# Soft-MoE tail of an attention kernel: the last two blocks of combine weights built before the first expert product, and half of the second expert layer issued in 16-instruction parts between the output tiles

## The chip, the core and the metric

The kernel runs on one core of a Trainium2 chip. The core has a tensor engine (PE; its weight loads are listed apart as PEld), a vector engine (DVE), a scalar engine (ACT), a general engine (POOL), and a queue engine (SP) that issues the kernel's transfers to 16 DMA engines. Each engine works through its own instructions in program order; engines wait for one another through semaphores. The metric is the device time of one execution in microseconds (us).

## The reference

Eight batches of eight heads, 576 tokens of 64 features. A causal softmax attention is mixed with a memory read-out by a gate; the result, 4608 rows of 512, goes into a soft mixture of experts: 8 experts, 4 slots each, hidden width 1024. What the change touches is only the end of it:

```python
logits = x @ phi                                  # 4608 x 32
d = softmax over the rows; slot_input = d.T @ x   # 32 x 512
for e in range(E):
    h = np.maximum(slot_input[e] @ w1[e], 0.0)    # 4 x 1024
    slot_out[e] = h @ w2[e]                       # 4 x 512
c = softmax of logits over the 32 slots           # the combine weights
return c @ slot_out                               # 4608 x 512
```

## The kernel before

The first nine tenths of the span run the attention pair by pair and, beside it, the running softmax of the slots. This part is a list of some thousand small steps in a fixed order (`SEQ`); `pin()` ties each engine's instructions to that order, so no planner moves anything. The change leaves this list alone.

The tail begins when the list is through. All of its matrices are small in rows and large in weights, so that it is a stream of expert weights through PE, and then a stream of output tiles to memory:

- `f1(eg, f)` (matmuls on line 937, ReLU on line 940) is one of four quarters of the first layer: expert group `eg` (4 experts), half `f` of the hidden width. 32 matmul instructions into one PSUM tile of the pool `psF` (2 buffers), then one ACT instruction.
- `f1t(eg, f)` (line 945) transposes its result on PE into a tile of `psP` (2 buffers); DVE copies it to `hT` (its row in the profile is the helper's line 357).
- `f2(dh, eg, f, cs_)` (line 954) is a quarter of the second layer for the output half `dh` (256 of the 512 columns), accumulated in one tile of `psF` over the four pairs (eg, f). `cs_` picks chunks of the hidden width: all four chunks are 32 matmul instructions, two are 16. So a quarter can be issued whole or in parts without a change in the instructions.
- `c1(qd)` (lines 960 to 971) makes the combine weights of row block `qd`: a transpose into `psP`, then a chain DVE, DVE, ACT exponential, four DVE. `c2(qd)` (line 975) transposes them back, and ACT copies them into `cT[:, qd]`. Blocks 0 to 6 were done in the list; 7 and 8 are left for the tail.
- `c3(i, j)` splits the combine weights into a high and a low part for the faster matmul type: two ACT casts (rows with the helper's line 354, `w<-cT` or `xk<-cT`) and one DVE subtraction (line 989). `c3(0, j)` takes 8 blocks at once (1024 columns), `c3(1, j)` only the ninth (128). The four tiles of `c3(0, j)` lie where weights of `f1(0, 1)` lay, so they may be written once that product has read them.
- `g1(dh)` (line 996, DVE) scales a finished half of the second layer; `g2(dh)` sums it over the partitions on PE (line 1000) and splits it (ACT cast, DVE line 1002).
- `comb(dh, t4)` makes one output tile of 512 rows by 256 columns: 4 matmuls (line 1011) into two tiles of `psC` (4 buffers), one copied out by ACT and one by DVE (`pc` in their rows), and a transfer of 512 KB to memory on the SP queue (line 1013). There are nine for each half.
- `wload` (line 757) loads one weight tile of 512 KB. 44 of 64 are loaded ahead of the tail; the other 20, all for the second layer, go into the buffers of first-layer weights that have been used (`reload`), so they wait for `f1(0, 0)`, `f1(0, 1)` and `f1(1, 0)`.

PE, ACT and DVE each take the tail's steps in the order of the lines 1015 to 1051: where a call stands in this list fixes the order of its instructions on every engine that it uses.

Of the kernel before, what the change touches and what calls it, by code (L numbers as in the profile page):

```python
# [284 lines left out]
def tile_attn_soft_moe(ctx, tc, q, k, v, M, beta, phi, w1, w2, cst, out):  # L285
# [67 lines left out]
    def act(o, i):  # L353
        nc.scalar.copy(o, i)  # L354
# [393 lines left out]
    def wload(x, pool, name):  # L748
        l, *i, g = order[x]


        if l == 0:
            t = pool.tile([128, 2, 512], F32, name=name)
            nc.sync.dma_start(out=t, in_=w1[4 * i[0] + g, i[1], i[2]])
        else:
            t = pool.tile([128, 4, 256], F32, name=name)
            nc.sync.dma_start(out=t, in_=w2[4 * i[1] + g, i[0], i[2]])
        wt[order[x]] = t
        wslot[order[x]] = (pool, name)
# [173 lines left out]
    def f1(eg, f):  # L933
        ps = psF.tile([128, 512], F32, name="pf")
        for c in range(4):
            for g in range(4):
                nc.tensor.matmul(ps[32 * g:32 * g + 32, :], si[:, c, 32 * (4 * eg + g):32 * (4 * eg + g) + 32],  # L937
                                 wt[0, eg, f, c // 2, g][:, c % 2, :], start=c == 0, stop=c == 3)
        h = hs[eg, f] = par[f].tile([128, 512], F32, name="qp")
        nc.scalar.activation(h, ps, AF.Relu)  # L940

    def f1t(eg, f):
        pt = psP.tile([128, 512], F32, name="pp")
        for x in range(4):
            nc.tensor.transpose(out=pt[:, 128 * x:128 * x + 128], in_=hs[eg, f][:, 128 * x:128 * x + 128], identity=ident)
        dve(hT[:, eg, 4 * f:4 * f + 4, :].rearrange("a x y -> a (x y)"), pt)


    def f2(dh, eg, f, cs_=range(4)):
        if dh not in po:  # L950
            po[dh] = psF.tile([128, 512], F32, name="pf")
        for c in cs_:
            for g in range(4):
                nc.tensor.matmul(po[dh][32 * g:32 * g + 32, 0:256], hT[:, eg, 4 * f + c, 32 * g:32 * g + 32], wt[1, dh, eg, f, g][:, c, :],  # L954
                                 start=(eg, f, c) == (0, 0, 0), stop=(eg, f, c) == (1, 1, 3))


    def c1(qd):
        ps = psP.tile([128, 512], F32, name="pp")
        nc.tensor.transpose(out=ps[:, 0:128], in_=y["lt"][:, qd - 7, :], identity=ident)  # L960
        lk = ps[:, 0:128].rearrange("a (j s) -> a j s", s=32)
        m4 = sml.tile([128, 4], F32, name="m4")
        nc.vector.reduce_max(out=m4, in_=lk, axis=AX.X)
        c = cc[qd] = sml.tile([128, 4, 32], F32, name=("lt", "ex")[qd - 7], bufs=1)
        nc.vector.tensor_tensor(out=c, in0=lk, in1=m4.rearrange("a (j x) -> a j x", x=1).broadcast_to([128, 4, 32]), op=ALU.subtract)
        nc.scalar.activation(c, c, AF.Exp)
        s4 = sml.tile([128, 4], F32, name="s4")
        nc.vector.reduce_sum(out=s4, in_=c, axis=AX.X)
        nc.vector.tensor_scalar(out=s4, in0=s4, scalar1=1e-9, scalar2=None, op0=ALU.add)
        nc.vector.reciprocal(out=s4, in_=s4)  # L970
        nc.vector.tensor_tensor(out=c, in0=c, in1=s4.rearrange("a (j x) -> a j x", x=1).broadcast_to([128, 4, 32]), op=ALU.mult)

    def c2(qd):
        ps = psP.tile([128, 512], F32, name="pp")
        nc.tensor.transpose(out=ps[:, 0:128], in_=cc[qd].rearrange("a j s -> a (j s)"), identity=ident)
        act(cT[:, qd, :], ps[:, 0:128])
# [4 lines left out]
    def c3(i, j):  # L981
        r = slice(32 * j, 32 * j + 32)
        if i == 0:
            pool, name = cslot[j]
            cst4.append(pool.tile([128, 8, 128], F32R, name=name))
        o, w = ((cst4[j], cT[r, 0:8]), (cst8[:, j], cT[r, 8]))[i]
        act(o[0:32], w)
        act(o[64:96], w)
        nc.vector.tensor_tensor(out=o[32:64], in0=w, in1=o[64:96].bitcast(F32), op=ALU.subtract)
# [5 lines left out]
    def g1(dh):  # L995
        nc.vector.tensor_scalar(out=ogs[:, dh], in0=po[dh][:, 0:256], scalar1=dt, scalar2=None, op0=ALU.mult)

    def g2(dh):
        pm = psP.tile([128, 512], F32, name="pp")
        nc.tensor.matmul(pm[:, 0:256], sel, ogs[:, dh], start=True, stop=True)  # L1000
        act(so[0:96, dh], pm[0:96, 0:256])
        nc.vector.tensor_tensor(out=so[64:96, dh], in0=pm[64:96, 0:256], in1=so[64:96, dh].bitcast(F32), op=ALU.subtract)

    def comb(dh, t4):
        pool, name = stage[NQ * dh + t4]
        o = pool.tile([128, 4, 256], F32, name=name)
        for half in range(2):
            ps = psC.tile([128, 2, 256], F32, name="pc")
            for v2 in range(2):
                u = 2 * half + v2  # L1010
                nc.tensor.matmul(ps[:, v2], (cst4[u][0:96, t4, :] if t4 < 8 else cst8[0:96, u, :]), so[0:96, dh], start=True, stop=True)  # L1011
            (act, dve)[half](o[:, 2 * half:2 * half + 2, :], ps)
        nc.sync.dma_start(out=out[512 * t4:512 * t4 + 512, 256 * dh:256 * dh + 256].rearrange("(u a) d -> a u d", a=128), in_=o)

    f1(0, 0)
    f1(0, 1)
    f1t(0, 0)
    c1(7)
    c1(8)
    f1(1, 0)  # L1020
    f1t(0, 1)
    c2(7)
    c2(8)
    f1(1, 1)
    f1t(1, 0)
    c3(0, 0)
    f2(0, 0, 0)
    f1t(1, 1)
    for x, (pool, name) in enumerate(reload):
        wload(nw + x, pool, name)  # L1030
    for j in range(1, 4):
        c3(0, j)
    for j in range(4):
        c3(1, j)
    f2(0, 0, 1)
    f2(0, 1, 0)
    f2(0, 1, 1)
    g1(0)
    f2(1, 0, 0, (0,))
    g2(0)  # L1040
    f2(1, 0, 0, (1, 2, 3))
    for t4 in range(NQ):
        comb(0, t4)
        if t4 == 4:
            f2(1, 0, 1)
    f2(1, 1, 0)
    f2(1, 1, 1)
    g1(1)
    g2(1)
    for t4 in range(NQ):  # L1050
        comb(1, t4)
    pin()
# [13 lines left out]
def build(nc, shapes=None):  # L1066
    dims = [("q", (B, 512, S + 384)), ("k", (B, 512, S)), ("v", (B, NP, 128, 6, 128)), ("M", (B, NP, 128, 160)),
            ("beta", (128, NP, 10)), ("phi", (128, NP, 32)),
            ("w1", (E, 2, 2, 128, 2, 512)), ("w2", (E, 2, 2, 128, 4, 256)), ("cst", (128, CW))]
    args = [nc.dram_tensor(f"in_{n}_dram", s, F32, kind="ExternalInput").ap() for n, s in dims]  # L1070
    args.append(nc.dram_tensor("out_0_dram", (B * S, DM), F32, kind="ExternalOutput").ap())
    with tile.TileContext(nc) as tc:
        tile_attn_soft_moe(tc, *args)
# [44 lines left out]
```

## Time and profile before

| | us |
|---|---|
| median of 3 runs | 483.08 (481.46 to 484.53) |
| the profiled execution, whole | 482.45 |
| its span, first to last instruction | 480.7 |
| start of the tail's first product `f1(0, 0)` | 416.01 |
| first output transfer issued | 450.95 |

The sum in the prediction is made against the profiled execution: what lies outside its span is 482.45 - 480.7 = 1.75 us, and the median of the runs is 0.63 us above it.

In the rows that follow, a line of the timeline has the start in us, the length in us, the engine, the line of the code, the operation, what is written from what is read, the shape, a count, and in brackets the idle time ahead of it with what ended it. A line with a count merges neighbours, and its length runs from the first one's start to the last one's end. In the chain of waits a line is start, length and what held up the end. In the table by stretches of time come the stretch, its length, the busy time of PE, PEld, DVE, ACT and POOL with instruction counts, the granted clock of PE as a share, the busy share of the DMA engines, and what they moved in GB/s.

### The profile page before, as it was taken

To read this page: it belongs to the slowest core of one execution; us is meant where nothing else is said; L and a number is where in the kernel's file an instruction comes from. 1 tells how busy PE (TensorE), PEld (TensorE's weight loads), DVE (VectorE), ACT (ScalarE), POOL (GpSimd) and SP (SyncE) were. 2 spreads that over 40 slices of the span, in tenths; PEclk is the share of its full clock that TensorE was granted. 3 is DMA by queue.
4 is the path that set the end of the run, shared out by engine and by line. 5 is a ranking of instruction groups with operands and counts; after the bars stand their busy time and mean duration, and the time that the engine had idled before them with its cause. 6 is when DMAs were issued, how large, how long until landed. Compare 5 with 4: busy or idle time off the path is not lost.

```text
span 480.7 us, 15438 instructions
## 1 busy us (share of the span) xinstructions
PE 431.5 (90%) x5762; PEld 288.1 (60%) x5762; DVE 378.3 (79%) x1289; ACT 341.2 (71%) x1001; POOL 168.8 (35%) x155
## 2 busy tenths in 40 slices
PE   7999999989999889999999989998889879897880
PEld 3666666756666666567567656665557646434550
DVE  6998898887987897899989998987899945335451
ACT  5988887778877786967879687786777943219340
POOL 1464456544525353255242544433345310000000
PEclk9999999999999999999999999999999999999895
DMA  7575386765567675756676677687875588699498
GB/s 259 152 204 163 114 243 192 216 195 146 157 190 238 209 222 166 203 155 181 192 218 199 179 234 243 202 261 169 222 202 145 157 275 285 244 412 410 154 342 312
DMA packets 65658, 104.09 MB, mean 217 GB/s; under 512 B 10608, under 2 KB 40880, under 8 KB 65584
## 3 DMA queue, kind: packets, MB, share of 16 engines
q1 hardware_dynamic: 65296, 103.02, 69.1%
q8 instruction: 46, 0.75, 0.6%
q14 instruction: 28, 0.23, 0.2%
q10 hardware_dynamic: 288, 0.09, 0.1%
HBM read 93.35 MB, written 9.73 MB: 214 GB/s over the span
## 4 chain that ended last, share of the span: by engine, by line
PE 32%; DMA 27%; DVE 21%; ACT 5%; POOL 5%; issue 4%; SPq 4%; DVEq 0%; POOLq 0%; ACTq 0%
DMA rb<-rd 10%; DMA rm<-rs 9%; PE psT L414 9%; DVE q L470 4%; PE psS L441 4%; PE psT L567 4%; PE pf L937 3%; DVE zq L470 3%; DMA rd<-rq 3%; DVE qp L519 2%; DVE at L357 2%; PE pc L1011 2%; ACT w L354 2%; POOL qp L557 2%; PE pf L954 2%
## 5 line engine op out<-in xcount | busy, mean ns | idle before, releaser
L414 PE MATMUL psT<-at,mv 128*32 128x64 f32 (+4 forms) x1536 | 103.4, 389 | 2.3 <-DMA mv<-in_v_dram 2.1
L354 ACT COPY at<-psT 128x256 f32<-128x256 f32 (+1 forms) x209 | 87.3, 481 | 23.9 <-PE psT L567 21.4
L478 ACT ACTIVATE q<-q,nm 128x384 f32<-128x384 f32 (+2 forms) x160 | 97.7, 614 | 8.4 <-DVE nm L470 5.7
L470 DVE CUSTOM_DVE_ANT_0 q<-psS,mv 128x512 f32<-128x512 f32 (+1 forms) x128 | 76.6, 612 | 5.0 <-PE psS L441 2.6
L441 PE MATMUL psS<-K,X 64*128 64x512 f32 (+2 forms) x576 | 72.3, 364 | 5.0 <-DVE nm L470 2.6
L567 PE MATMUL psT<-cs,q 128*128 128x128 f32 x480 | 70.0, 275 | 1.2 <-ACT q L478 0.6
L478 ACT ACTIVATE zq<-zq,nm 128x256 f32<-128x256 f32 (+2 forms) x128 | 68.0, 536 | 3.0 <-DVE nm L470 2.9
L441 PEld LDWEIGHTS psS<-K,X 64*128 64x128 f32 x576 | 45.2, 184 | 27.5 <-issue 9.5
L414 PEld LDWEIGHTS psT<-at,mv 128*32 128x32 f32 x1536 | 40.4, 110 | 32.6 <-issue 20.6
L567 PEld LDWEIGHTS psT<-cs,q 128*128 128x128 f32 x480 | 55.6, 141 | 4.0 <-issue 1.0
L557 POOL TENSOR_TENSOR qp<-qp,rb 128x576 f32<-128x576 f32 x23 | 33.5, 1458 | 53.1 <-DMA rb<-rd 39.0
L567 PE MATMUL psT<-cs,zq 128*128 128x128 f32 x288 | 46.8, 279 | 3.7 <-DVE xt L631 3.3
L512 POOL TENSOR_SCALAR qp<-qq 128x576 f32<-128x576 f32 x19 | 31.8, 1672 | 42.6 <-PE psT L414 41.2
L414 PE MATMUL psT<-qp,q 128*32 128x64 f32 (+1 forms) x512 | 37.3, 408 | 5.0 <-POOL qp L557 2.7
L567 PEld LDWEIGHTS psT<-cs,zq 128*128 128x128 f32 x288 | 34.1, 143 | 6.0 <-DVE xt L631 3.7
L409 POOL TENSOR_TENSOR K<-k,K 128x512 fp32r<-128x512 f32 x25 | 35.6, 1424 | 1.3 <-DVE K L357 0.4
L631 DVE TENSOR_TENSOR xt<-psT,rm 128x448 f32<-128x448 f32 (+7 forms) x60 | 23.6, 432 | 12.9 <-DMA rm<-rs 8.8
L414 PEld LDWEIGHTS psT<-qp,q 128*32 128x32 f32 x512 | 15.0, 109 | 31.0 <-issue 19.5
L357 DVE COPY at<-psT 128x512 f32<-128x512 f32 (+1 forms) x52 | 29.4, 585 | 4.6 <-PE psT L567 1.9
L359 POOL TENSOR_SCALAR K<-k 128x512 fp32r<-128x512 f32 x22 | 14.9, 675 | 50.6 <-PE psS L433 29.2
L519 DVE SCALAR_TENSOR_TENSOR qp<-qq,qp 128x576 f32<-128x576 f32 x32 | 31.1, 973 | 0.3 <-ACT qp L515 0.2
L478 ACT ACTIVATION_READ_ACCUMULATOR q<-q,nm 128x1 f32 x160 | 31.3, 196 | 0.0
(207 smaller groups left out, 796.5 us busy)
## 6 DMA issues: line engine op xcount, KB each, us to landing
w<-in_w_dram SPq DMA_DIRECT2D x49, 512.0 KB
qq<-in_q_dram SPq DMA_DIRECT2D x32, 480.0 KB
mv<-in_v_dram SPq DMA_DIRECT2D x32, 384.0 KB
k<-in_k_dram SPq DMA_DIRECT2D x32, 288.0 KB
rb<-rd SPq DMA_DIRECT2D x64, 144.0 KB
rm<-rs SPq DMA_DIRECT2D x64, 144.0 KB
q<-in_M_dram SPq DMA_DIRECT2D x32, 80.0 KB
out_dram<-w SPq DMA_DIRECT2D x5, 512.0 KB
```

Of the source, the lines that this page charges most:

```text
L354: nc.scalar.copy(o, i)
L357: nc.vector.tensor_copy(out=o, in_=i)
L409: ALU_ENG[ev("kl", n)].tensor_tensor(out=K2[:, 1, :], in0=st[n]["k"][:, 0:512], in1=K2[:, 0, :].bitcast(F32), op=ALU.subtract)
L414: nc.tensor.matmul(o[32 * g:32 * g + 32], w[:, 32 * g:32 * g + 32], x(g), start=start, stop=stop)
L441: nc.tensor.matmul(ps[:, c0:c0 + N], X[ROW[h], x, 128 * i - 128:128 * i], K2[ROW[h], y, 0:N], start=(x, y) == (0, 0), stop=(x, y) == (0, 1))
L470: nc.vector.tensor_tensor_reduce(out=sm, in0=src, in1=msk, op0=ALU.add, op1=ALU.min, scale=-0.125, scalar=m0, accum_out=acc_o)
L478: nc.scalar.activation(sm, sm, AF.Exp, scale=-1.0, bias=s["nm"][:, J:J + 1], accum_out=s["sum"][:, J:J + 1])
L512: ALU_ENG[ev("qmin", n)].tensor_scalar(out=st[n]["qp"], in0=st[n]["q"], scalar1=0.0, scalar2=None, op0=ALU.min)
L519: ALU_ENG[ev("qphi", n)].scalar_tensor_tensor(out=t, in0=st[n]["q"], scalar=0.0, in1=t, op0=ALU.max, op1=ALU.add)
L557: ALU_ENG[ev("qn", n)].tensor_tensor(out=s["qp"], in0=s["qp"], in1=s["rb"], op=ALU.mult)
L567: nc.tensor.transpose(out=ps[:, 128 * x:128 * x + 128], in_=src[:, k0:k0 + 128], identity=ident)
L631: nc.vector.tensor_tensor(out=o, in0=st[n]["oa"][:, c0:c1], in1=rr[:, 64 + c0:64 + c1], op=ALU.mult)
```

## The change

No computation is added or removed. The calls of the tail are put in another order:

1. `c1(7)` and `c1(8)` stand ahead of `f1(0, 0)`, and `c2(7)`, `c2(8)` between `f1(0, 0)` and `f1(0, 1)`. Before, they stood two quarters later each.
2. The four long splits `c3(0, j)` stand in pairs ahead of the third and the fourth quarter of the first layer, and with that ahead of their ReLUs on ACT. Before, they stood behind all four quarters. The four short splits `c3(1, j)` stay where they were.
3. Of the second half of the second layer, two chunks instead of one run between `g1(0)` and `g2(0)`, and none between `g2(0)` and the first `comb`. The remaining 14 chunks are cut into seven parts of two chunks (16 matmul instructions), one after each of the first seven output tiles of the first half. Before, three chunks stood ahead of the tiles, one quarter after the fifth tile, and two quarters after the ninth.
4. `g1(1)` stands after the seventh tile of the first half and its part, `g2(1)` after the eighth. Before, both stood after the ninth.

```diff
+    c1(7)
+    c1(8)
     f1(0, 0)
+    c2(7)
+    c2(8)
     f1(0, 1)
     f1t(0, 0)
-    c1(7)
-    c1(8)
+    c3(0, 0)
+    c3(0, 1)
     f1(1, 0)
     f1t(0, 1)
-    c2(7)
-    c2(8)
+    c3(0, 2)
+    c3(0, 3)
     f1(1, 1)
     f1t(1, 0)
-    c3(0, 0)
     f2(0, 0, 0)
     f1t(1, 1)
     for x, (pool, name) in enumerate(reload):
         wload(nw + x, pool, name)
-    for j in range(1, 4):
-        c3(0, j)
     for j in range(4):
         c3(1, j)
     f2(0, 0, 1)
     f2(0, 1, 0)
     f2(0, 1, 1)
     g1(0)
-    f2(1, 0, 0, (0,))
+    f2(1, 0, 0, (0, 1))
     g2(0)
-    f2(1, 0, 0, (1, 2, 3))
+
+    parts = [(0, 0, (2, 3)), (0, 1, (0, 1)), (0, 1, (2, 3)), (1, 0, (0, 1)), (1, 0, (2, 3)), (1, 1, (0, 1)), (1, 1, (2, 3))]
     for t4 in range(NQ):
         comb(0, t4)
-        if t4 == 4:
-            f2(1, 0, 1)
-    f2(1, 1, 0)
-    f2(1, 1, 1)
-    g1(1)
-    g2(1)
+        if t4 < 7:
+            f2(1, *parts[t4])
+        if t4 == 6:
+            g1(1)
+        if t4 == 7:
+            g2(1)
     for t4 in range(NQ):
         comb(1, t4)
     pin()
```

## The prediction, made before the changed kernel had run

> **What bounds the kernel now.** I read the page first, then the chain of waits over the last 85 us, then stretches of time with what the DMA engines moved, then the timeline of each engine in the tail.
>
> ```profile
> PE 431.5 (90%) x5762; PEld 288.1 (60%) x5762; DVE 378.3 (79%) x1289; ACT 341.2 (71%) x1001; POOL 168.8 (35%) x155
> out_dram<-w SPq DMA_DIRECT2D x5, 512.0 KB
> ```
>
> PE looks like the bound, but that is an average over a span whose first 416 us the change doesn't touch. The tail has a different limit. Its chain of waits:
>
> ```profile
> 416.01 7.07 PE pf L937 x64
> ...
> 434.03 0.92 ACT w L354
> ...
> 444.58 0.30 ACT xk L354
> ...
> 444.90 0.28 DVE xk L989
> ...
> 445.22 0.50 DVE k L996
> ...
> 445.76 0.70 PE pp L1000 x2
> 446.46 2.72 PE pf L954 x24
> 449.17 1.92 PE pc L1011 x10
> ```
>
> From 434 to 445 the chain is on ACT: the splits (c3). The scaling g1 on line 996 stands behind the last of them on DVE, though its own input was ready before; then g2 (L1000), 24 matmuls of the second half, and only then the first output tile (L1011). What the output waits on afterwards is seen in the stretches and the SP queue:
>
> ```profile
> 419.00:420.00 1.00, 1.00 (x16) 0.44 (x12) 0.00 (x0) 0.23 (x1) 0.00 (x0) 1.00 0.75 160
> ...
> 420.00:445.00 25.00, 21.06 (x252) 9.09 (x243) 11.40 (x24) 13.82 (x24) 0.00 (x0) 1.00 1.02 410
> 445.00:446.00 1.00, 0.24 (x1) 0.24 (x2) 0.67 (x2) 0.00 (x0) 0.00 (x0) 1.00 0.15 57
> 446.00:449.50 3.50, 3.50 (x28) 1.44 (x28) 0.42 (x1) 0.37 (x1) 0.00 (x0) 0.56 0.05 16
> 451.00:452.00 1.00, 0.93 (x7) 0.73 (x7) 0.99 (x2) 0.88 (x3) 0.00 (x0) 1.00 0.09 31
> 452.00:466.00 14.00, 12.29 (x136) 8.09 (x136) 6.93 (x12) 5.50 (x11) 0.00 (x0) 1.00 1.02 338
> 463.00:469.00 6.00, 5.38 (x34) 4.46 (x34) 4.84 (x8) 4.51 (x8) 0.00 (x0) 1.00 1.04 350
> 468.00:478.00 10.00, 1.53 (x10) 1.07 (x8) 2.25 (x4) 1.65 (x3) 0.00 (x0) 0.61 1.09 384
> 478.00:479.00 1.00, 0.00 (x0) 0.00 (x0) 0.00 (x0) 0.00 (x0) 0.00 (x0) 0.50 0.41 142
> ...
> 450.95 4.77 SPq L1013 DMA_DIRECT2D out_dram<-w  x5
> ...
> 464.88 0.37 SPq L1013 DMA_DIRECT2D out_dram<-X  x1
> ```
>
> The DMA engines carry the weights from 419.6 (0.6 of a full microsecond's bytes missing from 419 to 420) until 445.2, are empty for some 6 us, and from 451.9 on carry output without a gap until 478.4. One output is 512 KB = 0.524 MB. Nine at 338 GB/s take 13.96 us, so the first half ends near 465.9; the second half was issued from 464.88, about a microsecond ahead of that, and nine more at 384 GB/s take 12.29 us. So **after the first output the tail is bound by the transfers of the output**: 451.9 + 13.96 + 12.29 = 478.15, and 2.55 us later the span ends. What can be gained is an earlier first output, as long as the transfers then never run dry.
>
> **The change part by part.** The rows for it:
>
> ```profile
> 423.02 0.66 PE L945 MATMUL pp<-cs,qp 128*128 128x128 f32 x4
> 423.51 0.27 PE L960 MATMUL pp<-cs,rb 128*128 128x128 f32 x1
> 424.45 0.33 PE L960 MATMUL pp<-cs,rb 128*128 128x128 f32 x1 [0.68 <-DVE at L357]
> 424.71 3.64 PE L937 MATMUL pf<-w,at 128*32 128x512 f32 x32
> 428.29 0.66 PE L945 MATMUL pp<-cs,qp 128*128 128x128 f32 x4
> 429.66 2.33 PE L937 MATMUL pf<-w,at 128*32 128x512 f32 x17
> 433.24 0.66 PE L945 MATMUL pp<-cs,qp 128*128 128x128 f32 x4
> 439.75 2.34 PE L954 MATMUL pf<-w,at 128*32 128x256 f32 x40
> 445.76 0.70 PE L1000 MATMUL pp<-k,cs 128*128 128x256 f32 x2 [3.67 <-DVE k L996]
> 454.66 2.04 PE L1011 MATMUL pc<-k,w 96*128 96x256 f32 x12
> 456.53 1.00 PE L1011 MATMUL pc<-k,xk 96*128 96x256 f32 x4
> 457.46 3.66 PE L954 MATMUL pf<-w,at 128*32 128x256 f32 x64
> 461.73 0.70 PE L1000 MATMUL pp<-k,cs 128*128 128x256 f32 x2 [0.61 <-DVE k L996]
> 463.34 5.70 PE L1011 MATMUL pc<-k,w 96*128 96x256 f32 x32 [0.91 <-DVE k L1002]
> ...
> 415.97 0.16 DVE L886 RECIPROCAL dt<-dt 128x1 f32<-128x1 f32 x1
> 424.32 0.28 DVE L963 TENSOR_REDUCE m<-pp 128x4 f32<-128x128 f32 x1
> 427.96 0.29 DVE L971 TENSOR_TENSOR ex<-ex,s 128x128 f32<-128x128 f32 x1
> ...
> 433.43 0.60 ACT L940 ACTIVATE qp<-pf 128x512 f32<-128x512 f32 x1 [3.40 <-PE pf L937]
> 433.93 8.44 ACT L354 CAST w<-cT 32x1024 fp32r<-32x1024 f32 x8
> 442.39 2.48 ACT L354 CAST xk<-cT 32x128 fp32r<-32x128 f32 x8
> ```
>
> (1) c1 and c2 leave their old places. Between the f1t at 423.02 and the next f1 at 424.71 lie 1.69 us, of which f1t's four transposes take 0.49 (to 423.51): 1.2 come free. Between 428.29 and 429.66 it is 1.37 - 0.5 = 0.87. Sum: 2.07 us off PE.
>
> (2) Their new places. The two c1 transposes (0.3 us each) fall into the 0.67 us in which PE waits for DVE ahead of 416.01: nothing, at most 0.3. The DVE chain of both blocks takes 424.32 to 428.25 = 3.93 us; behind the reciprocal at 415.97 it runs from about 416.05 to 420.0, on a DVE and an ACT that were idle then. f1(0,0) ends at 416.01 + 7.07/2 = 419.55, so c2(8) waits for the chain, and f1(0,1) starts after its transpose (0.33) at about 420.35: a cost of 0.8. Net so far 2.07 - 0.8 = 1.27 us: f1(1,1) ends at 432.0 instead of 433.24. Reloads that wait for f1(0,1) are issued 0.8 us later on SP; eight of 0.524 MB at 410 GB/s (10.2 us) are queued ahead of them, so the engines don't run dry and the weights still end at about 445.2. No other transfer moves past them.
>
> (3) The long casts: eight in 8.44 us, 1.055 each, two pairs (4.22 us) ahead of each of the last two ReLUs. f1(0,1) ends at 423.95; ReLU 0.60, four casts to 428.8. f1(1,0) ends at about 428.1, so its ReLU is 0.7 late; nothing needs it until f1t(1,0) at 432.0. Four casts more to 433.5; the ReLU of f1(1,1) is 1.4 late and ends at 434.1. Its transposes stand behind f2(0,0,0), which covers until 432.5 + 1.83 = 434.3 (32 at 3.66/64). So both are hidden, the second by only 0.2 us; with that cover gone it costs what is beyond it, up to the 4.22 of a stage. DVE's copies behind the subtractions are late too (f1t(0,1) until 430.7, f1t(1,0) until 435.4), ahead of the f2 that reads them. The short splits end at 434.1 + 2.48, their subtractions by 438: g1(0) no longer waits for them.
>
> (4) f2(0,\*): before, the 40 matmuls from 439.75 (0.058 each) end near 442.1, eight of them of the other half, so the first half was complete at 441.63. Now it is at 440.4. g1 (0.50) is covered by the 16 matmuls (0.93), g2 starts at 441.3 instead of 445.76. From g2 to the first comb it is 1.61 us where nothing stands between (461.73 to 463.34), against 3.41 before: comb(0,0) at **442.9 instead of 449.17**. From there to the issue 1.54 (463.34 to 464.88): the first output at 444.45 instead of 450.95, **6.5 us earlier**, its data from 445.4, right behind the weights.
>
> (5) The interleaving. A tile takes PE 1.87/12 x 4 = 0.62 us (12 matmuls started from 454.66 to 456.53; 0.71 by the row of 32), a part 3.66/64 x 16 = 0.92: 1.54 to 1.63 a round, I take 1.58. The transfer of a tile takes 0.524/338 = 1.55. So PE and DMA are nearly equal in these seven rounds. The eighth tile is issued at 442.9 + 11.06 + 1.54 = 455.5, 0.2 behind the transfers; the ninth behind it (g2's 0.70 between) in time. The first half is through at 459.55. g2(1) starts near 454.6, comb(1,0) at 456.2 to 456.8, its data at 458.7 to 459.3: in time by 0.2 to 0.8. Then 12.29 + 2.55 gives an end at 474.4.
>
> Sum: -6.5 + 0.2 = **-6.3 us**: 480.7 becomes 474.4, 482.45 becomes 476.15, and from the median 483.08, **476.8**. The floor of this mechanism is 445.2 + 26.25 + 2.55 = 474.0, or 476.4: the weights themselves stand ahead of the output.
>
> A price with two values: at which rate do the weights come? The row says 410 GB/s from 420 to 445. The Trainium skill (DMA: Bandwidth & Descriptors, Specifications) gives an HBM limit of about 358 GB/s for a core. By that, as an estimate, twenty weights would last until 419.6 + 29.3 = 448.9, the output could begin only there, and the gain would be some 3 us (about 480). The row decides: 410 was reached in this very stretch, and neither the count nor the order of the weights changes.
>
> **The rivals.**
>
> *Starved transfers.* If a round takes more than 1.58 us, seven rounds add up: at 1.91 it is 2.3 us, **479.1**. For it: 0.2 us of slack, and the first tiles from 449.17 on took 1.92/10 x 4 = 0.77 each, the clock still low for a part of it. Against it: 0.62 at full clock.
>
> *Casts on the chain.* The change only moves ACT's 8.44 us from behind the ReLUs to between them. If PE waits for each group of casts, it loses up to 4.2 us and the gain is 2.1: **481.0**. Against it: a stage of f1 lasts 3.6 us on PE, ReLU and one pair 2.7; but the four casts stand in one group of 4.22, and the cover is 0.2. [...]
>
> *Slower: PE at half clock through the rounds.* After the idle 3.67 us ahead of 445.76 the row of 446 to 449.5 has a clock of 0.56. If the clock fell because of the short gaps at tile boundaries and stayed at half, a round would take 3.1 us, comb(1,0) would come at 468, its data at 471.1, and the span would end at 486.0: **488.4**. It decides from a round of 2.6 us on, where the second half's data comes later than 465.9. Against it: at 463 to 469, tiles only, with gaps of 0.61 and 0.91 just before, the clock was 1.00. The Trainium skill (TensorE: Matmul & The Clock Gate, A second HAM failure mode) tells of such a fall where matmul groups cycle through PSUM buffers with small pauses. No row here shows it for pauses under a microsecond.
>
> **How the numbers follow.** Forecast 0.70 (its own range 475 to 478.6), starved 0.14, casts 0.11, half clock 0.05. The three runs lie 1.6 below and 1.45 above their median. The range goes from the floor less that, 476.4 - 1.5 = 474.9, to the starved case plus that, 479.1 + 1.45, rounded to 480.6. About 1% (4.8 us) is what a measurement of this kernel tells from no change. Faster by more: nearly all of the forecast and some of the starved case, 0.73; within 1%: the rest and the casts, 0.23; slower: 0.04.
>
> **What would show it.** Right: g1 on line 996 released by PE and not by the splits, first output issued near 444.5, no empty microsecond of DMA between weights and output, 338 GB/s kept until about 459.5, PE clock 1.00 to the end of the tiles. Step 2 is wrong if f1(0,1) starts after 421, step 3 if f1t(1,1) waits for ACT, step 5 if the rate between 446 and 460 falls under 320. The whole forecast is wrong if the rates of 338 and 384 belong not to the halves of the output but to what the engines do at the time: the same 9.44 MB at 338 throughout would end 1.7 us later.

## The result, and the profile after

| | before | after |
|---|---|---|
| median of 20 runs each, us | 484.20 (479.12 to 488.43) | 477.37 (473.39 to 484.39) |
| ratio after / before, 95% interval | | 0.9877 (0.9847 to 0.9908) |
| the profiled execution, whole / span, us | 482.45 / 480.7 | 484.39 / 482.6 |
| start of `f1(0, 0)` in it, us | 416.01 | 424.01 |
| first output issued, us after that start | 34.94 | 28.65 |
| first output issued to the end of the span, us | 29.75 | 29.94 |
| the tail: start of `f1(0, 0)` to the end of the span, us | 64.69 | 58.59 |

The change makes the kernel about 1.2% faster. The ratio leaves out the slow executions, those more than 1.5% above the fastest of their kernel. The profiled execution of the changed kernel is its longest run: its attention part, which both kernels share, ended 8 us later. So all comparisons of traces below go by the tail, counted from the start of `f1(0, 0)`, which waits for the same DVE result (line 885) in both kernels. The tail is 6.1 us shorter.

The chain of waits of the changed kernel (start, length, what held up the end):

```profile
428.19 0.30 PE pp L975
428.49 3.57 PE pf L937 x32
...
440.37 0.59 PE pp L945 x4
440.96 1.86 PE pf L954 x32
442.82 0.59 PE pp L945 x4
443.41 6.18 PE pf L954 x112
449.59 0.64 PE pp L1000 x2
...
450.26 0.38 ACT k L354
...
450.66 0.43 DVE k L1002
...
451.13 0.73 PE pc L1011 x4
451.87 1.00 PE pf L954 x16
452.87 0.67 PE pc L1011 x4
```

From 428 to 450 the chain is PE without a break. Before, it lay on ACT's casts and DVE's subtraction from 434 to 445. The reader should also see what is *not* in it: no `w L354`, no `xk L989`. The timeline of the changed kernel has the same work by engine:

```profile
424.01 3.64 PE L937 MATMUL pf<-w,at 128*32 128x512 f32 x32 [0.39 <-DVE dt L885]
428.42 3.64 PE L937 MATMUL pf<-w,at 128*32 128x512 f32 x32
442.75 0.66 PE L945 MATMUL pp<-cs,qp 128*128 128x128 f32 x4
451.13 0.73 PE L1011 MATMUL pc<-k,w 96*128 96x256 f32 x4 [0.91 <-DVE k L1002]
452.80 0.74 PE L1011 MATMUL pc<-k,w 96*128 96x256 f32 x4
462.83 0.74 PE L1011 MATMUL pc<-k,w 96*128 96x256 f32 x4
465.12 5.70 PE L1011 MATMUL pc<-k,w 96*128 96x256 f32 x32 [0.44 <-DVE k L1002]
...
448.80 0.48 DVE L996 TENSOR_SCALAR k<-pf,dt 128x256 f32<-128x256 f32 x1 [3.06 <-PE pf L954]
...
437.55 4.22 ACT L354 CAST w<-cT 32x1024 fp32r<-32x1024 f32 x4
441.79 0.60 ACT L940 ACTIVATE qp<-pf 128x512 f32<-128x512 f32 x1
...
452.66 7.06 SPq L1013 DMA_DIRECT2D out_dram<-w  x5
```

DVE has stood idle for 3.06 us ahead of the scaling on line 996, and PE's product releases it: the splits are no longer ahead of it. Between the two last ReLUs the four casts take 4.22 us, and PE's transposes at 442.75 start 0.36 us after the ReLU has ended, since PE was still at work before them: the casts are hidden. The stretches of the changed kernel (length, busy time of the five engines, granted clock, DMA share, GB/s):

```profile
429.00:452.00 23.00, 22.09 (x266) 9.66 (x258) 9.66 (x15) 13.07 (x21) 0.00 (x0) 1.00 1.03 411
...
453.00:454.00 1.00, 1.00 (x16) 0.69 (x19) 0.42 (x1) 0.59 (x1) 0.00 (x0) 1.00 0.44 161
454.00:468.00 14.00, 13.45 (x140) 8.64 (x132) 7.99 (x13) 6.60 (x12) 0.00 (x0) 1.00 0.96 321
470.00:480.00 10.00, 1.29 (x8) 0.84 (x7) 2.01 (x4) 1.42 (x3) 0.00 (x0) 0.68 1.09 384
```

The six empty microseconds of DMA are gone: one microsecond at 161 GB/s lies between the last weight and the first output. But the first half of the output goes at 321 GB/s, not at 338.

### The profile page after: what moved, and what is told of

Read it like the earlier page. It is cut to its first block, busy times and chain, and to the rows that moved or that the text cites. A ratio compares the mean times of both kernels' runs of the same rounds, so it can differ in the third digit from the quotient of the medians.

```text
span 482.6 us, 15440 instructions
## 1 busy us (share of the span) xinstructions
PE 430.4 (89%) x5762; PEld 286.7 (59%) x5762; DVE 381.2 (79%) x1289; ACT 341.6 (71%) x1001; POOL 168.2 (35%) x155
## 4 chain that ended last, share of the span: by engine, by line
PE 32%; DVE 28%; DMA 27%; issue 4%; SPq 3%; POOL 3%; ACT 1%; DVEq 0%; POOLq 0%; ACTq 0%
PE psT L414 11%; DMA rb<-rd 9%; DMA rm<-rs 9%; DVE q L470 5%; PE psS L441 4%; DVE zq L470 4%; DMA mv<-in_v_dram 4%; DVE qp L519 3%; PE pf L954 3%; DMA rd<-rq 3%; PE psT L567 2%; PE pf L937 2%; PE pc L1011 2%; DVE at L357 2%; DVE X L403 2%
## 5 line engine op out<-in xcount | busy, mean ns | idle before, releaser
L354 ACT COPY at<-psT 128x256 f32<-128x256 f32 (+1 forms) x209 | 87.3, 481 | 22.6 <-PE psT L567 20.1
L567 PE MATMUL psT<-cs,zq 128*128 128x128 f32 x288 | 45.8, 275 | 2.7 <-DVE xt L631 2.5
L414 PE MATMUL psT<-qp,q 128*32 128x64 f32 (+1 forms) x512 | 38.3, 416 | 6.6 <-POOL qp L557 3.3
L519 DVE SCALAR_TENSOR_TENSOR qp<-qq,qp 128x576 f32<-128x576 f32 x32 | 33.2, 1037 | 0.3 <-ACT qp L515 0.2
L433 PE MATMUL psS<-K,X 128*128 128x256 f32 x192 | 31.1, 297 | 0.3 <-POOL X L403 0.3
```

Of the source, the lines that this page charges most:

```text
L414: nc.tensor.matmul(o[32 * g:32 * g + 32], w[:, 32 * g:32 * g + 32], x(g), start=start, stop=stop)
L433: nc.tensor.matmul(o, X[:, x, 448:576], K2[:, y, x0:x1], start=(x, y) == (0, 0), stop=(x, y) == (0, 1))
L519: ALU_ENG[ev("qphi", n)].scalar_tensor_tensor(out=t, in0=st[n]["q"], scalar=0.0, in1=t, op0=ALU.max, op1=ALU.add)
L567: nc.tensor.transpose(out=ps[:, 128 * x:128 * x + 128], in_=src[:, k0:k0 + 128], identity=ident)
```

## The experiments

The clock of PE was half for some 3.4 us of `f1(0, 0)` in seven of the fourteen profiles, whichever kernel it was (row of 413 to 417 below). That costs 1.56 to 1.70 us of the tail where `f1(0, 1)` follows at once (8.63 to 8.77 against 7.07 for 64 matmuls) and 1.20 to 1.23 us where the combine weights stand between them, since a wait for DVE hides a part of it there (`f1(0, 1)` starts 5.60 to 5.64 instead of 4.40 or 4.41 us after `f1(0, 0)`). The table has it taken off the tail in brackets where it was so; the first output is given as it was. Each ratio is against runs of the kernel before on the same chip.

| run | first output after start | tail (corrected) | time or ratio |
|---|---|---|---|
| before, again | 34.94 | 64.79 | 484.32 us, one run |
| `r1_c1c2_only` | 35.15 | 65.06 (63.83) | 0.9989 (0.9942 to 1.0037) |
| `r2_c1c2c3` | 28.93 | 58.77 | 0.9863 (0.9812 to 0.9915) |
| `r3_parts_only` | 35.60 | 67.70 (66.0) | 1.0061 (1.0021 to 1.01) |
| `r4_swap_halves` | 28.92 | 58.87 | 476.44 us, one run |
| `r5_reverse_buffers` | 30.14 | 60.28 (59.05) | 484.75 us, one run |
| `r6_parts_warm` | 34.58 | 64.48 (62.79) | 1.004 (0.9978 to 1.0101) |
| `r7_late_first_tile` | 31.24 | 61.21 | 482.76 us, one run |
| `r8_aligned` | 28.92 | 57.67 | 483.22 us, one run |
| `r9_all_misaligned` | 30.15 | 60.52 (59.29) | 477.02 us, one run |
| `r10_gap_aligned` | 29.87 | 58.46 (57.26) | 0.9772 (0.9707 to 0.9836) |
| `r11_before_aligned` | 37.20 | 66.13 (64.57) | 0.9962 (0.9924 to 1.0) |

The single times scatter with the attention part (`f1(0, 0)` starts between 413.14 and 424.01), so only the tails of those runs are compared.

**The kernel before once more**, to see how far a tail repeats.

> The kernel before once more, to see how far one profile repeats. Tail length is counted from the start of the first product f1(0,0) to the end of the span: 64.69 us before, 58.59 us after. All theories: 64.7 within 0.3, although the start of f1(0,0) itself may move by several us with the attention part ahead of it.

Its tail is 64.79 against 64.69, its first output 34.94 after the start both times. Differences of a few tenths of a microsecond in a tail mean something only where a row shows where they come from.

**Which part of the change carries the gain.** First the combine weights' early place alone, on the kernel before:

```diff
+    c1(7)
+    c1(8)
     f1(0, 0)
+    c2(7)
+    c2(8)
     f1(0, 1)
     f1t(0, 0)
-    c1(7)
-    c1(8)
     f1(1, 0)
     f1t(0, 1)
-    c2(7)
-    c2(8)
```

> Only c1 and c2 moved. Theory (the end follows the first output, and the splits c3 on ACT are what keeps the first output late): PE reaches the end of f1(1,1) about 0.95 to 1.27 earlier, ACT's splits start and end that much earlier, first output about 1 us earlier: tail 63.5 to 63.8. PE still idles some 3.7 us ahead of g2 and its clock still falls to a half behind that. Rival (c1 and c2 carry most of the gain): tail under 61.

Timeline of this run, then one of its stretches:

```profile
413.14 5.34 PE L937 MATMUL pf<-w,at 128*32 128x512 f32 x32 [0.39 <-DVE dt L885]
418.78 3.64 PE L937 MATMUL pf<-w,at 128*32 128x512 f32 x32
...
443.19 0.70 PE L1000 MATMUL pp<-k,cs 128*128 128x256 f32 x2 [3.67 <-DVE k L996]
```

```profile
413.00:417.00 4.00, 3.86 (x21) 1.29 (x25) 2.88 (x14) 0.62 (x2) 0.00 (x0) 0.57 0.03 10
```

PE still idles 3.67 us ahead of line 1000, as before the change: the casts stand behind the last ReLU, and the chain through them only begins as much earlier as PE got done earlier. The tail is 0.9 us shorter with the half clock taken off; the ratio (0.9942 to 1.0037) can't tell that from no change. Now both moves of combine weights and splits, with the second half in the old large pieces (the changed kernel less its parts 3 and 4):

```diff
     g1(0)
-    f2(1, 0, 0, (0, 1))
+    f2(1, 0, 0, (0,))
     g2(0)
+    f2(1, 0, 0, (1, 2, 3))
     for t4 in range(NQ):
         comb(0, t4)
-        if t4 < 7:
-            f2(1, *parts[t4])
-        if t4 == 6:
-            g1(1)
-        if t4 == 7:
-            g2(1)
+        if t4 == 4:
+            f2(1, 0, 1)
+    f2(1, 1, 0)
+    f2(1, 1, 1)
+    g1(1)
+    g2(1)
```

> c1, c2 and the long splits c3 moved, the second half of the second layer in its old order (one chunk ahead of g2(0), three behind it, a quarter after the fifth tile, two after the ninth). Theory: the wait on the splits is gone, the 24 matmuls behind g2(0) fill the gap in which PE would wait anyway, first tile about 27.3 us after the start of f1(0,0) (27.12 in the changed kernel, 33.16 before); the transfers never run dry: tail 58.6 within 0.4, the same as the changed kernel. Rival (the small parts between the tiles carry a part of the gain): tail 60 or more.

```profile
421.93 3.64 PE L937 MATMUL pf<-w,at 128*32 128x512 f32 x32 [0.39 <-DVE dt L885]
...
447.26 0.70 PE L1000 MATMUL pp<-k,cs 128*128 128x256 f32 x2 [0.17 <-DVE k L996]
...
449.32 3.45 PE L1011 MATMUL pc<-k,w 96*128 96x256 f32 x20
...
450.86 4.96 SPq L1013 DMA_DIRECT2D out_dram<-w  x5
```

In this timeline the idle time ahead of line 1000 is 0.17 us instead of 3.67, and the tail (58.77) is that of the whole change (58.59). So **the splits ahead of the ReLUs, with the combine weights' move as their condition, are the whole gain** as far as these runs tell (by the tails, 0.9 of the 5.9 us came with the combine weights alone). The splits alone could not be tried: `c3` needs blocks 7 and 8 of the combine weights, so their move has to come first.

The other half alone, on the kernel before (parts 3 and 4 of the change as in its diff, parts 1 and 2 left out):

> Only the second half of the second layer in small parts, with g1(1), g2(1) early; c1, c2, c3 in their old places. Theory: g1(0) still waits for the splits at 29.2 us after the start of f1(0,0), PE idles about 3.2 us; first tile 1.8 earlier than before, first output 1.9 earlier. At full clock the tail is 63.0; if the clock falls to a half behind the idle time as it did before, the first rounds are longer than a transfer and the tail is 64.0 to 64.7. Rival (small parts carry the gain): tail under 61.

Timeline, then stretches, of this run:

```profile
418.20 8.77 PE L937 MATMUL pf<-w,at 128*32 128x512 f32 x64 [0.67 <-DVE dt L885]
...
449.65 1.22 PE L1000 MATMUL pp<-k,cs 128*128 128x256 f32 x2 [3.24 <-DVE k L996]
...
451.78 1.22 PE L1011 MATMUL pc<-k,w 96*128 96x256 f32 x4 [0.91 <-DVE k L1002]
...
454.80 1.22 PE L1011 MATMUL pc<-k,w 96*128 96x256 f32 x4
...
456.99 0.74 PE L1011 MATMUL pc<-k,w 96*128 96x256 f32 x4
...
458.66 0.74 PE L1011 MATMUL pc<-k,w 96*128 96x256 f32 x4
```

```profile
450.00:456.00 6.00, 5.09 (x30) 2.64 (x33) 1.11 (x2) 1.32 (x3) 0.00 (x0) 0.50 0.22 76
...
460.00:468.00 8.00, 7.56 (x81) 4.68 (x74) 4.18 (x8) 3.20 (x6) 0.00 (x0) 1.00 0.90 302
```

The small parts alone lose, by 0.2 to 1.0%. Behind the idle 3.24 us the clock is 0.50, from 449.3 to 456.1 by the trace's clock records; the first two rounds then take 3.0 and 2.2 us (451.78 to 454.80 to 456.99) instead of 1.67, and from 450 to 456 DMA carries 76 GB/s. How long the clock stays low there is not set by the order alone: it was 3.4 us in the kernel before, in its repetition and in `r1_c1c2_only`, and 6.8 us in this run and in `r11_before_aligned`, which has the old order. To see whether the clock is the cause, 28 matmul calls (56 instructions) whose result nothing reads keep PE busy through that wait:

```diff
     f2(1, 0, 0, (0, 1))
+    idle = psC.tile([128, 2, 256], F32, name="pc")
+    for i in range(7):
+        for g in range(4):
+            nc.tensor.matmul(idle[32 * g:32 * g + 32, 0], hT[:, 0, i, 32 * g:32 * g + 32], wt[1, 0, 0, 0, g][:, i % 4, :], start=True, stop=True)
     g2(0)
```

> The kernel of r3 (small parts only, c1, c2, c3 in their old places) with 28 more matmul calls on PE, of no use to the output, put between the parts and g2(0): 3.2 us of work of f2's kind, into the idle time in which PE waits for the splits. Theory (r3 lost because the idle time lets the clock fall to a half, and rounds of 3.0 and 2.2 us then starve the transfers): the clock stays at 1.00, all rounds 1.67, the first tile at the same place, 2 us of starving gone: tail, with the first product at full clock, 63.5 to 64.3 instead of 66.0, time 1.5 to 2.5 us under r3. Rival (the interleaving itself starves the transfers at any clock): no change against r3.

```profile
449.06 0.70 PE L1000 MATMUL pp<-k,cs 128*128 128x256 f32 x2 [0.21 <-DVE k L996]
...
450.68 0.73 PE L1011 MATMUL pc<-k,w 96*128 96x256 f32 x4 [0.91 <-DVE k L1002]
...
452.34 0.74 PE L1011 MATMUL pc<-k,w 96*128 96x256 f32 x4
```

With PE busy, line 1000 takes 0.70 instead of 1.22 and the first round 1.66 instead of 3.02: the corrected tail is 3.2 us shorter than without the 28 calls. So in the profiles the loss of the parts alone is the half clock. The times don't show it: the ratios, 1.0061 and 1.004, have intervals that overlap. Whether the parts then beat the kernel before is not settled either: by the one profile the corrected tail is 1.9 us shorter, but a gain of 1.9 us would be a ratio of 0.996, outside the interval (0.9978 to 1.0101). Uncorrected the tail is 0.2 us shorter, which lies inside it.

**Is the first output the right thing to gain?** The same device, 24 such calls ahead of `g2(0)` in the changed kernel, puts nothing late but the first tile and what follows it:

```diff
     f2(1, 0, 0, (0, 1))
+    idle = psC.tile([128, 2, 256], F32, name="pc")
+    for i in range(6):
+        for g in range(4):
+            nc.tensor.matmul(idle[32 * g:32 * g + 32, 0], hT[:, 0, i, 32 * g:32 * g + 32], wt[1, 0, 0, 0, g][:, i % 4, :], start=True, stop=True)
     g2(0)
```

> The changed kernel with 24 more matmul calls (48 instructions, 2.77 us, of no use to the output) on PE ahead of g2(0), at full clock and with everything else in place. It changes only when the first tile is made. Theory (the end follows the first output): first output 2.77 later (31.4 us after the start of f1(0,0) instead of 28.65), tail 61.3 to 61.5 instead of 58.59. Rival (the order of the parts or the weights set the end): tail under 60.

The first output is issued 2.59 us later after the start than in the changed kernel (31.24 against 28.65), and the tail is 2.62 us longer (61.21 against 58.59). The end follows the first output one for one.

**To whom do the rates of 338 and 384 GB/s belong?** The prediction took them for the two halves of the output and named this as what could bring it down. Two edits of `r2_c1c2c3`, which like the kernel before carries nine tiles slowly and nine fast: the two halves of the columns change places in memory (so the first nine tiles go where the last nine went), or the staging buffers are taken in reverse.

```diff
-        nc.sync.dma_start(out=out[512 * t4:512 * t4 + 512, 256 * dh:256 * dh + 256].rearrange("(u a) d -> a u d", a=128), in_=o)
+        nc.sync.dma_start(out=out[512 * t4:512 * t4 + 512, 256 - 256 * dh:512 - 256 * dh].rearrange("(u a) d -> a u d", a=128), in_=o)
```

> The kernel of r2 with the two column halves of the output exchanged at the transfer: the first nine tiles go to columns 256 to 511, the last nine to 0 to 255 (so the output has its halves exchanged). It asks what the two rates of the output are due to: 338 GB/s for the first nine tiles and some more, 384 for the rest. If to the destination columns: 384 first, then 338. If to the buffers they are sent from, or to the order in time: as before, 338 first, 384 from about 14 to 15 us after the first data. Tail 58.8 within 0.4 in the two latter cases; up to 1.6 longer in the first, since the second half's first tile would come after the transfers ran dry.

```diff
-    stage = [wslot[order[x]] for x in range(4 + len(order) - nw, 22 + len(order) - nw)]
+    stage = [wslot[order[x]] for x in range(4 + len(order) - nw, 22 + len(order) - nw)][::-1]
```

> The kernel of r2 with the 18 output buffers used in reverse order. If the rate belongs to the buffer (fast ones were those of the last eight tiles), the first eight tiles now go at 384 and the rest at 338, with an empty stretch of 1 to 2 us before the second half: tail 60 to 60.5. If it belongs to the order in time or to the destination: 338 first, 384 later, tail 58.8 within 0.4.

Stretches of the run with exchanged halves, then of the one with reversed buffers:

```profile
446.00:460.00 14.00, 12.27 (x137) 8.11 (x135) 6.84 (x11) 5.51 (x11) 0.00 (x0) 1.00 1.03 340
462.00:471.00 9.00, 1.28 (x8) 0.83 (x6) 2.01 (x4) 1.41 (x3) 0.00 (x0) 0.76 1.09 384
```

```profile
454.00:464.00 10.00, 9.30 (x120) 5.88 (x118) 4.54 (x8) 3.04 (x6) 0.00 (x0) 1.00 1.08 378
466.00:468.00 2.00, 1.91 (x12) 1.48 (x11) 1.98 (x3) 1.90 (x4) 0.00 (x0) 0.94 0.38 130
469.00:481.00 12.00, 3.89 (x17) 3.36 (x16) 3.46 (x5) 2.63 (x5) 0.00 (x0) 0.50 1.03 341
```

The destination changes nothing. With the buffers reversed, the first nine go at 378 GB/s while PE is as busy as ever, and the last nine at 341 while it is busy for a third of the time: the rate is the buffer's, and has nothing to do with what the engines do. What tells the buffers apart is where they begin in a partition. In the program as built, the first ten of `r2_c1c2c3` begin 96 or 128 bytes past a multiple of 256, and of the last eight only two. The intervals between the first data of one tile and of the next, in us (a tile is 512 packets of 1 KB, so the start of every 512th packet in the trace is taken):

```
tile                    2     3     4     5  ...   11    12    15    16    17
r2_c1c2c3             1.49  1.51  1.54  1.54      1.37  1.36  1.36  1.36  1.36
r5_reverse_buffers    1.43  1.37  1.36  1.39      1.53  1.54  1.57  1.53  1.50
r8_aligned            1.36  1.36  1.36  1.36      1.36  1.36  1.36  1.36  1.36
r9_all_misaligned     1.49  1.51  1.54  1.54      1.53  1.54  1.56  1.54  1.49
```

The last two are the test. Padding of 160 bytes and two widths rounded up to a multiple of 256 bytes make every output buffer begin at such a multiple; 96 bytes ahead of the others make every one miss it, by 96 or 224 bytes (both on `r2_c1c2c3`):

```diff
     dt = const.tile([128, 1], F32, name="dt")
+    fill = const.tile([128, 40], F32, name="fill")
+    nc.vector.memset(fill, 0.0)
...
-    rm = spl.tile([128, 1060], F32, name="rm")
+    rm = spl.tile([128, 1088], F32, name="rm")
...
-    SMW = {"q3": 1024, "q2": 1056, "zq": 1152}
+    SMW = {"q3": 1024, "q2": 1088, "zq": 1152}
```

> The kernel of r2 with 160, 112 and twice 128 bytes of padding per partition, so that all 18 output buffers begin at a multiple of 256 bytes. Theory (a transfer of 1 KB pieces from a buffer that does not begin at such a multiple is slower): all tiles at 380 to 386 GB/s, the first nine through after 12.3 us, then an empty stretch of 1 to 2 us before the second half's first tile, tail 58.2 to 58.8. Rival (the rate belongs to the place of a buffer in memory or to the order): 338 for the first ten again, no empty stretch, tail 58.8.

```diff
     par = [ctx.enter_context(tc.tile_pool(name=f"par{i}", bufs=1)) for i in range(2)]
+    fill = par[0].tile([128, 24], F32, name="fill")
+    nc.vector.memset(fill, 0.0)
```

> The kernel of r2 with 96 bytes of padding ahead of the buffers that were fast, so that none of the 18 output buffers begins at a multiple of 256 bytes. Theory (alignment): 330 to 350 GB/s for all 18 tiles, about 27.9 us for all of them, tail 60.2 to 60.6. Rival (place or order): 384 for the last eight again, tail 58.8 within 0.4.

Stretches, first of the aligned run, then of the other:

```profile
454.00:464.00 10.00, 9.30 (x118) 5.66 (x117) 4.44 (x7) 2.83 (x5) 0.00 (x0) 1.00 1.09 385
466.00:467.00 1.00, 1.00 (x7) 0.78 (x7) 1.00 (x2) 0.90 (x3) 0.00 (x0) 1.00 0.07 25
468.00:478.00 10.00, 3.11 (x19) 2.40 (x18) 3.78 (x6) 2.92 (x5) 0.00 (x0) 0.83 1.09 385
```

```profile
447.00:460.00 13.00, 11.29 (x130) 7.39 (x123) 6.05 (x10) 4.78 (x10) 0.00 (x0) 0.99 1.02 340
461.00:472.00 11.00, 3.98 (x17) 3.45 (x16) 3.51 (x6) 2.72 (x5) 0.00 (x0) 0.50 1.02 342
```

Both halves at 385, or both at 340 to 342, with nothing else changed: the alignment of a run of buffers decides. It isn't the whole rule, though. `rm`, the source of the seventeenth tile, begins 96 bytes past a multiple of 256 in `r2_c1c2c3` as well as in the misaligned run, and takes 1.36 us in the first, between aligned ones, and 1.49 in the second, between others like itself. Of the 1.6 us that nine faster tiles are worth (9 x 0.18), the aligned run's tail gains 1.1: now the second half is late, and DMA is nearly empty from 466 to 467 (25 GB/s). The tails alone would not have decided: the corrected ones of the reversed and of the misaligned run are 59.05 and 59.29, where 60 to 60.6 was expected, and that of the aligned run 57.67, where 58.2 to 58.8 was. All three are shorter than expected, and step 5 below shows what these expectations left out.

**A version that uses both.** With aligned buffers a tile takes 1.36 us of DMA, and the rounds of tile and part (1.67) are too long. One part is moved into the wait between `g2(0)` and the first tile, where PE has nothing to do, and the parts begin behind the second tile; the padding is that of the aligned run:

```diff
     g2(0)
-    parts = [(0, 0, (2, 3)), (0, 1, (0, 1)), (0, 1, (2, 3)), (1, 0, (0, 1)), (1, 0, (2, 3)), (1, 1, (0, 1)), (1, 1, (2, 3))]
+    f2(1, 0, 0, (2, 3))
+    parts = [(0, 1, (0, 1)), (0, 1, (2, 3)), (1, 0, (0, 1)), (1, 0, (2, 3)), (1, 1, (0, 1)), (1, 1, (2, 3))]
     for t4 in range(NQ):
         comb(0, t4)
-        if t4 < 7:
-            f2(1, *parts[t4])
+        if 0 < t4 < 7:
+            f2(1, *parts[t4 - 1])
```

> The changed kernel with the aligned buffers of r8 and with the first of the seven parts moved between g2(0) and the first tile (into the 0.91 us in which PE waits there) and the six others one tile earlier in number, none after the first tile. Theory: first output where it was (28.6 us after the start of f1(0,0)), tiles at 1.36 us each where they are ready, PE's rounds of 1.67 now the longer ones; the first half is through about 13.3 us after its first data and the second half follows at once: tail 57.4 to 57.9, 0.7 to 1.2 us under the changed kernel. Rival (alignment is of no use): tail 58.3 to 58.7.

```profile
446.00:452.00 6.00, 6.00 (x80) 3.42 (x78) 2.68 (x4) 2.35 (x4) 0.00 (x0) 1.00 1.08 383
452.00:458.00 6.00, 5.56 (x50) 3.94 (x43) 4.04 (x8) 3.14 (x7) 0.00 (x0) 1.00 0.94 330
459.00:470.00 11.00, 3.34 (x21) 2.57 (x20) 3.87 (x7) 3.06 (x6) 0.00 (x0) 0.83 1.09 385
```

The stretches show 383 GB/s until the two tiles' lead is used up, 330 while PE's rounds set the pace, and 385 to the end; from 446 to 471 no microsecond carries less than 284 GB/s. Its median is 473.2 us (470.5 to 476.86, six runs) against 485.67 for the kernel before, the ratio 0.9772 (0.9707 to 0.9836). Its interval lies wholly below that of the change (0.9847 to 0.9908): by the ratios it beats both kernels. Its tail is shorter than that before by 7.4 us, while the ratio stands for 8.0 to 14.2 us. Whether the padding also helps the attention part was tried on the kernel before:

> The kernel before with the aligned buffers of r8 and nothing else changed, to see what alignment is worth without the change. In the tail: all tiles at 380 to 386 GB/s, but the second half's first tile is no earlier, so that the transfers run dry for 1 to 2 us ahead of it; tail 64.0 to 64.7 instead of 64.69 (at full clock in the first product). Theory A (alignment counts only in the output): time within 0.3% of before. Theory B (the loads of the attention part gain too, which would explain that r10's time lies 4 us under the changed kernel's, with a tail only about 1.3 shorter): time 0.5 to 1% under before, and the tail as in A.

The kernel before gains 0 to 3.7 us from the padding (0.9962, 0.9924 to 1.0), with a corrected tail of 64.57 against 64.69 and 64.79 without it. So the corrected tail gains next to nothing, but in this profile the clock is at half for 6.8 us behind the idle stretch instead of 3.4, and the first output comes 0.7 us later than before (37.20 - 1.56 = 35.64 us after the start). From there to the end it is 28.93 us against 29.75: there the padding gains 0.8 us, and more is lost because the faster first half waits for the second (DMA carries 24 GB/s from 465 to 466). Whether the attention part gains from the padding stays open.

## Why the prediction was right, point by point

The forecast was 476.8 us (474.9 to 480.6), and 477.37 was measured.

| step | predicted | measured |
|---|---|---|
| 1: off PE | 2.07 us | 1.89 |
| 2: `f1(0, 1)` behind the start of `f1(0, 0)` | 4.34 us (0.8 late) | 4.41 (0.88 late) |
| 1 and 2: `f1(1, 1)` ends earlier by | 1.27 us | 0.94 |
| 3: cover of the last group of casts | 0.2 us | 0.36 |
| 4: first tile after the start | 26.9 us | 27.12 |
| 4: first output earlier by | 6.5 us | 6.29 |
| 5: a round of tile and part | 1.58 us | 1.67 |
| 5: first output to the end, against before | +0.2 us | +0.19 |
| sum | -6.3 us | -6.10 |

**Steps 1 and 2.** The two `c1` transposes cost nothing, as said: PE's idle time ahead of `f1(0, 0)` only shrinks from 0.67 to 0.39 us. `c2(8)` does wait for the DVE chain, and the wait is the price expected. The net gain is a quarter smaller than the sum (0.94 against 1.27 us): 0.18 us less came free on PE, the wait is 0.08 us longer, and 0.07 us are lost elsewhere.

**Step 3** decides, and holds: the mechanism is shown by the rows of lines 996 and 945 and by the run without the small parts. The rival with the casts on the chain (481.0) is refuted: no ReLU of the first layer holds up PE.

**Step 4.** The first output comes 6.29 us earlier and stands right behind the weights, and the end moves with it (`r7_late_first_tile`). The weights came at 411 GB/s. By the rule of the Trainium skill weighed there (DMA: Bandwidth & Descriptors, Specifications; about 358 GB/s from memory for a core) they would, as an estimate, have ended 3.7 us later (448.9 against 445.2 on the clock of the kernel before). The measurement decides against the rule for this kernel.

**Step 5 is the mis-sized term.** Between the tiles at 451.13 and 462.83 lie seven rounds of 1.67 us, not 1.58: the chain has 0.67 for a tile and 1.00 for a part, where 0.92 was taken from rows of 64 matmuls in a row. A round is thus longer than a slow transfer (1.55), and the rate falls to 321 GB/s from 454 to 468. Counted from the start of `f1(0, 0)` this is the stretch in which the prediction would have called its step wrong under 320 GB/s; so it stands by one GB/s, and the 338 that it forecast until 459.5 was not kept. The rival of starved transfers is there in small: the last tile's first data come 25.95 us after the first tile's, 0.8 later than before (25.15).

That the end still lies only 0.19 later, as forecast, is luck and no merit of the sum: from the first output data to the last it is 27.52 to 27.71 us in the five runs with the old pieces and these buffers in this order, where the last tile begins at 25.13 to 25.16, and 27.76 and 27.77 in the changed kernel and `r7_late_first_tile`, where it begins at 25.95. A last tile that begins later is through faster (1.81 instead of 2.37 to 2.58 us). The packets show where the time lies. In those five runs fewer than four packets are under way at a time in the last 1.0 to 1.2 us, where some 16 are before: one to three of the 16 DMA engines end late and alone. In the changed kernel that lasts 0.34 us, and in the runs with reversed, misaligned and aligned buffers 0.07, 0.28 and 0.38. So the old order ends with most of a microsecond that no step names, and the changed kernel saves it while it loses 0.8 us by starving. The expectations for the three buffer runs started from a tail of 58.8 that contains it, and came out too long. An engine that has fallen behind still has work while the others wait, which would explain why the starving costs nothing; that it is so isn't shown, since the traces don't give the DMA engine of a packet.

**The slower rival**, PE at half clock through the rounds because of the short gaps between tiles, did not come to pass: the clock is 1.00 from 454 to 468. Half clock in the rounds occurred in `r3_parts_only`, but behind an idle stretch of 3.24 us and for the first two rounds only. Parts 1 and 2 of the change take that stretch away; without them the same rounds lose time.

**What the prediction did not see** is that parts 3 and 4 of the change bring nothing (58.59 against 58.77). Step 4 put a gain of 1.8 us on them, since no matmuls of the second half stand between `g2(0)` and the first tile any more (1.61 us instead of 3.41). In `r2_c1c2c3` 24 of these still stand there, and it is 2.06 us (447.26 to 449.32) at full clock: 1.35 of the 1.8 us were the half clock behind the idle stretch, which part 2 takes away. And where step 5 took the small parts for the way to keep DMA fed, the old large pieces keep it as full (338 and 384 GB/s in the kernel before, intervals of 1.49 to 1.54 and 1.36 us in `r2_c1c2c3`). Its warning about 338 and 384 GB/s put the question to the engines; the answer is the buffers' alignment, which is the same before and after, so the sum was not touched by it. The floor named with the sum is not one: with aligned buffers the best version's tail is 57.3 us, below the 58.0 of that floor (474.0 less 416.01), with the half clock taken off.

## What to carry to other kernels

An engine that is 90% busy over the span can be idle where the end is decided: read the chain of waits of the last stage, and put work whose input is ready (here the casts) where its engine is waiting anyway, as long as other work of the engine behind it covers the delay. Cutting work small to feed the transfers brought nothing here where the large pieces kept them fed (a tail of 58.59 against 58.77), and behind an idle stretch of 3.24 us, with the clock at half in the profile, the same cut cost 0.2 to 1.0%. And where a transfer rate changes between two like streams, exchange the buffers before blaming the engines.

## What the runs showed of the hardware that was not expected

**Alignment of the source.** Transfers of 512 KB in packets of 1 KB from a row of on-chip buffers that begin 96 or 128 bytes past a multiple of 256 take 1.49 to 1.61 us, mostly 1.54, and 1.36 us from those that begin at one (340 to 342 against 385 GB/s), a factor of 1.13. The Trainium skill (DMA: Bandwidth & Descriptors, How a descriptor splits into AXI transactions) has each transaction begin at a multiple of 256 bytes; worked out from it as an estimate, a packet 96 or 128 bytes off would take 35 or 36 beats of 32 bytes instead of 32, a factor of 1.09 or 1.13, and one 224 bytes off 39, a factor of 1.22. The runs agree in direction. But the three buffers of the misaligned run that begin 224 bytes off take 1.53 to 1.58 us, no more than their neighbours, and single misaligned buffers between aligned ones cost almost nothing (intervals of 1.36 and 1.39 us in `r2_c1c2c3`, 1.39 and 1.43 in `r5_reverse_buffers`). So the count of beats isn't the whole cause, and what else is stays open.

**The clock.** Behind the idle stretches of 3.2 to 3.7 us it was half for 3.41 us (the kernel before, its repetition, `r1_c1c2_only`) or for 6.83 us (`r3_parts_only`, `r11_before_aligned`), by the trace's clock records. It was also half for 3.41 us at `f1(0, 0)` in half of the profiles, with 0.39 or 0.67 us of idle time just ahead; no run tells why. In the second half of the tiles it fell to half in five of the nine runs with the old pieces in the old places, among them those with reversed and with misaligned buffers (0.50 in their last stretches), behind the same gaps of 0.61 and 0.91 us after which the kernel before kept 1.00. It cost nothing there that the tails show (58.77 with it in `r2_c1c2c3`, 58.87 without it in `r4_swap_halves`), because the transfers set the end.
